# Odd transforms summed from PSUM and block evictions moved between engines, in a Fourier transform with a feed-forward layer behind it

## The chip, the cores and the metric

One core of a Trainium2 chip runs the whole kernel. The metric is the device time of one execution in microseconds. Engines by the names of the profile: PE (TensorE, products), DVE (VectorE), ACT (ScalarE), POOL (GpSimd), and SP, whose queue issues most of the transfers.

## The reference

```python
X = np.fft.fft(x, axis=1)             # x: 8 batches x 3072 positions x 256 features, float32
X = np.fft.fft(X, axis=2).real
h = X.reshape(8 * 3072, 256) @ w_in   # 256 x 2048
g = np.maximum(h, 0.0) + alpha * np.minimum(h, 0.0)
y = g @ w_out                         # 2048 x 256
```

So the real part of a transform over positions and features, a layer of 2048 hidden features with a slope of its own for each below zero, and a layer back to 256.

## The kernel before, in words

The transform over positions is folded by its symmetries into short cosine and sine products. For each of 8 batches, the input is first folded by sums and differences (`fold_piece`, four pieces on POOL and two on DVE), and then four even units (`unit`) and two odd units (`unit_odd`) make the values X that the layers read. X is kept as a high and a low part, four rows of 1552 columns: cosine high, cosine low, sine high, sine low. The transform over features is multiplied into w_in at the start.

An odd unit makes two transforms of two halves each, every one in a bank of PSUM (`dft`). ScalarE copies the second half of a bank to `os` (`odd_sums`), DVE adds and subtracts `os` and the first half (`both_sums`, L526), and three more operations of DVE combine the two results (L552, L554). `to_x` then writes the high part with ScalarE and the low part with POOL. For the sine unit, one row also goes to DRAM (`xcd`), to be spread over all partitions later.

The layers run in blocks of 512 columns (386 or 384 in the first and last batch). A block has 16 steps, one for each 128 hidden features. `step(s)` issues `ffn1(s + 3)` (six products into two banks), `ffn2(s)` (twelve products that accumulate in four banks, `acc[o, i]`), and `pair(s + 3)`, which turns the two banks of ffn1 into rows with their slope: DVE L697, L705 and L652, ScalarE L709 and L658 (high part), POOL L660 (low part). Each product is split in high and low parts, so three products stand for one. The first 14 steps of all do the weights too.

Four banks, in a ring (`pq`), serve ffn1, the transforms and the weights; the ring gives a bank to its next user when the last reader of the older contents is done. The other four are `acc`. Every engine works through its instructions in the order in which this code issues them.

At the last step of a block, `evacuate(g, 0)` is issued before `pair`, and `evacuate(g, 1)` behind it: ScalarE copies `acc[0, *]` and DVE `acc[1, *]` to SBUF, and SP sends each half out. In that last step ffn2 finishes acc 0 first and acc 1 in its second half. In all other steps, the first of the next block among them, its order is

```python
order = [(0, woh, H), (0, wol, H), (1, wol, H), (1, woh, H), (1, woh, L), (0, woh, L)]   # (o, weights, part), each for i = 0, 1
```

so the first product that writes acc 1 is the fifth, and the sixth writes `acc[1, 1]`.

X takes the place of a tile with inputs of the start (`before`). At row 3 of batch 0, POOL clears seven columns of all four rows of X (L906). In batch 0 the odd units stand at rows 16 and 19 (a row is one step), the fold of the next batch goes from row 20 to row 50; in the other batches the odd units stand at rows 0 and 3 and the fold goes from row 4 to 36. Towards the end of each batch `turn_rows` and `mids` prepare the operands of the next odd units, on ScalarE and POOL.

Of the kernel before, what the change touches and what calls it, by code (L numbers as in the profile page):

```python
# [9 lines left out]
F32 = mybir.dt.float32  # L10
# [7 lines left out]
ALU = mybir.AluOpType  # L18

NB, N, D, DFF = 8, 3072, 256, 2048  # L20
P = 128
KF = DFF // P
W = 384
WX = 386
WM = 512
XS, X0 = 1552, 7
SINGLE = 1537
BLOCKS = [(0, 0, 386), (0, 386, 384), (0, 770, 384), (0, 1154, 384)]
# [10 lines left out]
def _halves(v):  # L39

    return v.rearrange("p (h a) -> p a h", h=2)


def _pairs(v):

    return v.rearrange("p (a h) -> p a h", h=2)


def _place(b, kind):

    return {"ee": 0, "eo": 385, "o": 769}[kind[1:]] + (b == 0 and kind[1:] != "ee")
# [65 lines left out]
def _columns(b):  # L117

    j, i2 = np.arange(193), np.arange(192)
    n = 193 if b == 0 else 192  # L120
    i3 = np.concatenate([767 - 2 * j, 2 * j[:192], 768 - 2 * j[1:], 2 * j[1:192] - 1])
    k = [4 * (384 - j), 4 * j[:n], 4 * i2 + 2, 4 * (383 - i2) + 2, 2 * i3 + 1]
    sign = [-np.ones(193), np.ones(n), np.ones(192), -np.ones(192), (-1.0) ** i3]
    return np.concatenate(k), np.concatenate(sign)
# [9 lines left out]
def fft2_prelu_ffn(ctx: ExitStack, tc: tile.TileContext, t, outputs):  # L134
    nc = tc.nc
# [5 lines left out]
    foldp = ctx.enter_context(tc.tile_pool(name="foldp", bufs=1))  # L141
# [8 lines left out]
    st = start.enter_context(tc.tile_pool(name="st", bufs=1))  # L150

    V, S, G = nc.vector, nc.scalar, nc.gpsimd
# [9 lines left out]
    r128 = small.tile([1, NB], F32, name="r128")  # L162
    before = xp.tile([P, 4, XS], F32, tag="X", name="before")
    dummy = work.tile([P, 512], F32R, tag="hi0", name="dummy", bufs=3)
# [15 lines left out]
    xcd = dram.tile([NB, 1544], F32, name="xcd")  # L180
# [71 lines left out]
    wpart, w32 = {}, {}  # L252
# [40 lines left out]
    whole = st.tile([P, KEPT, D], F32, name="whole")  # L293
# [219 lines left out]
    def odd_sums(ps, n, m):  # L513
        os = foldp.tile([P, 193], F32, tag="os", name="os", bufs=2)[0:m, 0:n]
        S.activation(out=os, in_=ps[:, n:2 * n], func=ACTF.Copy)  # L515
        return ps, os, n, m

    def butterfly(ps, n, m, last=None):
        return both_sums(*odd_sums(ps, n, m), last=last)

    def both_sums(ps, os, n, m, pool=foldp, tag="y", last=None):
        wide, bufs = (WM, 1) if tag == "pf" else (WX, 2)
        last = last or n
        y = pool.tile([P, wide], F32, tag=tag, name="y", bufs=bufs)[0:m, 0:n + last]
        for i, (op, k) in enumerate(((ALU.subtract, n), (ALU.add, last)) if n == 193 else ((ALU.add, n), (ALU.subtract, n))):
            V.tensor_tensor(out=y[:, i * n:i * n + k], in0=ps[:, 0:k], in1=os[:, 0:k], op=op)  # L526
        return y

    def mids(b, nm):
# [7 lines left out]
    def mid_of(nm, i):  # L537
        return [m[:, i * P:(i + 1) * P] for m in middle[nm]] if nm in middle else None

    def unit_odd(b, nm, whole=True):  # L540

        z = zres[:, 1 if nm == "co" else 2]
        ps = [
            dft("ca", fold[b, "a" + nm], z, P, mid_of(nm, 0)), dft("sb", fold[b, nm][:, 3:6], None, P, mid_of(nm, 1)),
        ]
        parted = [(s, i, *split_sum(s, i)) for s, i in list(st1)]
        sums = [odd_sums(*v) for v in ps]
        for v in parted:
            split_parts(*v)
        ya, yb = (both_sums(*v, last=192) for v in sums)  # L550
        y = [foldp.tile([P, 512], F32, tag="xe" + e, name="yo")[:, 0:385] for e in "vg"]
        V.tensor_tensor(out=y[0], in0=ya, in1=yb, op=ALU.add)  # L552
        for o, n, at in ((0, 192, 1), (192, 191, 194)):
            V.tensor_tensor(out=y[1][:, o:o + n], in0=ya[:, at:at + n], in1=yb[:, at:at + n], op=ALU.subtract)  # L554
        at = _place(b, nm)
        for o, v in ((0, y[0]), (385, y[1][:, 0:383])):
            if nm == "so":
                nc.sync.dma_start(out=xcd[b:b + 1, at + o:at + o + v.shape[-1]], in_=v[0:1])
            to_x(0 if nm == "co" else 2, at + o, v, G)

    def unit(b, kind, lo_engine):
        sums = unit_mm(b, kind, pq.tile([P, 512], F32, tag="pq", name="ps"))
# [5 lines left out]
    def unit_mm(b, kind, bank=None):  # L568
        nm, o = kind[0] + "e", 0 if kind[1:] == "ee" else 3
        zr = zres[:, 0] if kind == "cee" else None  # L570
        return dft(kind, fold[b, nm][:, o:o + 3], zr, P, mid_of(nm, o // 3), bank)

    def unit_store(b, kind, lo_engine, y):
        s, at = 0 if kind[0] == "c" else 2, _place(b, kind)
        to_x(s, at, y if kind[1:] == "eo" or b == 0 else y[:, 0:385], lo_engine)
        if kind == "cee" and 0 < b < NB - 1:
            c = X0 + SINGLE + b
            lo_engine.tensor_copy(out=X[:, 0:2, c:c + 1], in_=X[:, 0:2, X0:X0 + 1].bitcast(F32))

    def to_x(s, c, v, lo_engine):  # L580
        hi, lo = (X[:, s + i, X0 + c:X0 + c + v.shape[-1]] for i in range(2))
        S.activation(out=hi, in_=v, func=ACTF.Copy)
        lo_engine.tensor_tensor(out=lo, in0=v, in1=hi.bitcast(F32), op=ALU.subtract)
# [86 lines left out]
    def ffn1(s):  # L670
# [4 lines left out]
        for q in range(2):  # L675
            t_ = pq.tile([P, 512], F32, tag="pq", name="pq")[:, 0:w]
            xh, xl = X[:, 2 * q, c:c + w], X[:, 2 * q + 1, c:c + w]
            xh, xl, out = _halves(xh), _halves(xl), _pairs(t_)
# [54 lines left out]
    acc = {}  # L733
# [34 lines left out]
    def evacuate(g, o):  # L768
        b, c, w = BLOCKS[g]
        if o == 0:  # L770
            outs[g] = outp.tile([P, 2, 2, w], F32, tag="o", name="o")
        v = outs[g]
        dst = outputs[g]
        for i in range(2):
            if o == 0:
                S.activation(out=v[:, o, i], in_=acc[o, i], func=ACTF.Copy)  # L776
            else:
                V.tensor_copy(out=v[:, o, i], in_=acc[o, i])
        nc.sync.dma_start(out=dst[:, o], in_=v[:, o])

    outs = {}
# [46 lines left out]
    sums = {0: fold_sums(0)}  # L828
# [21 lines left out]
    weights_b(1)  # L850
    weights_m(1, G)
    X = xp.tile([P, 4, XS], F32R, tag="X", name="X")
    see_sums = unit_mm(0, "see")
    cee_sums = unit_mm(0, "cee")
    x_sums = odd_sums(*x_sums)
# [4 lines left out]
    y = both_sums(*see_sums)  # L860
# [3 lines left out]
    y = both_sums(*cee_sums)  # L864
# [30 lines left out]

    for b in range(NB):
        mine = [g for g, block in enumerate(BLOCKS) if block[0] == b]
        r_odd, r_fold, r_end = (16, 20, 50) if b == 0 else (0, 4, 36)
        beside = []
        for r in range(len(mine) * KF):  # L900
            s = mine[0] * KF + r
            g, f = divmod(s, KF)
            step(s)
            if b == 0:
                if r == 3:
                    G.memset(X[:, :, X0 + SINGLE:X0 + SINGLE + 7].bitcast(F32), 0.0)  # L906
                    nc.sync.dma_start(out=er, in_=t["er"])
                if r == 9:
                    column_128_store("ceo", butterfly(*column_128_mm("ceo")))
                if r in (10, 11):  # L910
                    unit(0, ("ceo", "seo")[r - 10], G)
                if r in (12, 13):
                    if r == 13:
                        fold_128(0)
                    turn_rows(0, ("co", "so")[r - 12])
                if r == 25:
                    start.close()
                    late = ctx.enter_context(tc.tile_pool(name="late", bufs=1))
                if r in TABLE_STEPS:
                    parts_table(list(TABS)[TABLE_STEPS.index(r)])  # L920
            if f == 10:
                load_xbc(g + 1)
            q = r - r_odd
            if q in (0, 3):
                unit_odd(b, ("co", "so")[q // 3])
            if b + 1 < NB:
                if r == r_fold:
                    fold_tiles(b + 1)
                for i, e, r0, r1 in FOLDS:
                    r0, r1 = (r_fold + round(v * (r_end - r_fold)) for v in (r0, r1))  # L930
                    if r == r0:
                        by = one_by_one if e is V else spread
                        beside.append(by(fold_whole(6 * b + 6 + i, e), r0, r1))
                for x in beside:
                    next(x, None)
                if r == r_end + 1:
                    fold_rows(b + 1)
                    fold_128(b + 1)
                for nm, at in zip(("se", "ce", "co", "so"), (51, 52, 60, 62) if b == 0 else (37, 37, 44, 46)):
                    if r == at:  # L940
                        if nm[1] == "o":
                            turn_rows(b + 1, nm)
                        mids(b + 1, nm)
                for kind, at in zip(("see", "cee", "ceo", "seo"), (53, 55, 57, 58) if b == 0 else (38, 40, 41, 42)):
                    if r == at:
                        unit(b + 1, kind, G)
# [64 lines left out]
```

## Time and profile before

| | before |
|---|---|
| median of 3 runs | 1674.95 us (1674.49 to 1676.68) |
| the profiled execution | 1675.75 us |
| its span, first to last instruction | 1673.9 us |
| PE busy | 1642.9 us (98%) |
| DVE busy | 1512.8 us (90%) |
| POOL busy | 1328.4 us (79%) |
| ACT busy | 1133.8 us (68%) |

The times in the rows below are those of the profiled execution, counted from the start of its span. Products overlap, and the end of each is modelled, so a PE that is shown busy need not be at its peak; starts are what one can count on. A wait is put down to the last thing that ended it.

### The profile page before, as it was taken

The page shows a single profiled execution, that of the slowest core. Times are in us where ns is not written, and L with a number is a line of the kernel's source. Part 1 is how long each engine was busy: PE and PEld are TensorE (multiplying, and loading weights), DVE is VectorE, ACT ScalarE, POOL GpSimd, SP SyncE. Part 2 cuts the span into 40 slices and gives each one's busy share as a digit, 9 for nine tenths or more (in the row PEclk, how much of TensorE's full clock was granted, in tenths as well). Part 3 has the DMA queues.
Part 4 walks back from the last instruction along what each step waited for, and adds up shares of the span by engine and source line. Part 5 has one row for each costly group of instructions (what it writes and reads, how often), then busy time and mean ns, then how long its engine had stood idle before and what let it go on. Part 6 is the DMA issues. An engine that isn't in the chain of part 4 may idle for free.

```text
span 1673.9 us, 26326 instructions
## 1 busy us (share of the span) xinstructions
PE 1642.9 (98%) x8154; PEld 1462.0 (87%) x8154; DVE 1512.8 (90%) x2630; ACT 1133.8 (68%) x2094; POOL 1328.4 (79%) x1420
## 2 busy tenths in 40 slices
PE   8999999999999999999999999999999999999998
PEld 6778899888888888888888888888888888899998
DVE  7879998999889998999979998899988999889997
ACT  5876777666676666766676666766667666677775
POOL 2368997788878887889877898778887888776665
PEclk9999999999999999999999999999999999999999
DMA  6310120010100111001100111001010010000000
GB/s 237 134 62 6 58 69 20 7 70 26 45 26 20 57 39 33 32 24 47 67 3 32 39 45 57 26 7 70 29 42 26 20 45 31 1 31 25 25 20 20
DMA packets 25289, 69.93 MB, mean 42 GB/s; under 512 B 6174, under 2 KB 7486, under 8 KB 25150
## 3 DMA queue, kind: packets, MB, share of 16 engines
q1 hardware_dynamic: 24398, 67.80, 11.5%
q8 instruction: 65, 1.06, 0.3%
q14 instruction: 74, 0.61, 0.1%
q10 hardware_dynamic: 752, 0.45, 0.1%
HBM read 42.98 MB, written 25.25 MB: 41 GB/s over the span
## 4 chain that ended last, share of the span: by engine, by line
PE 88%; DVE 6%; POOL 2%; issue 2%; ACT 1%; DVEq 0%; POOLq 0%; ACTq 0%
PE acc L762 54%; PE pq L679 9%; PE pq L680 9%; PE pq L681 9%; PE ps L507 3%; DVE d L705 2%; PE ps L504 2%; PE acc L746 1%; DVE pf L697 1%; DVE d L652 1%; POOL lo L660 1%; PE fold L392 0%; PE ps L320 0%; DVE we L276 0%; DVE wm L280 0%
## 5 line engine op out<-in xcount | busy, mean ns | idle before, releaser
L660 POOL TENSOR_TENSOR lo<-d,hi 128x512 fp32r<-128x512 f32 (+2 forms) x804 | 973.2, 1227 | 238.8 <-ACT hi L658 234.8
L658 ACT ACTIVATE hi<-d 128x512 fp32r<-128x512 f32 (+2 forms) x804 | 482.7, 600 | 352.6 <-DVE d L652 254.0
L652 DVE SCALAR_TENSOR_TENSOR d<-d,sg,pq 128x512 f32<-128x512 f32 (+2 forms) x804 | 565.5, 703 | 11.1 <-ACT pq L709 11.1
L709 ACT ACTIVATE pq<-d,sga 128x512 f32<-128x512 f32 (+2 forms) x804 | 526.4, 656 | 48.8 <-DVE d L705 47.8
L705 DVE TENSOR_TENSOR d<-pf,pq 128x512 f32<-128x512 f32 (+2 forms) x832 | 531.1, 641 | 14.6 <-POOL lo L660 5.5
L762 PE MATMUL acc<-hi,woh 128*128 128x512 f32 (+2 forms) x1608 | 456.2, 365 | 1.5 <-ACT o L776 1.4
L762 PE MATMUL acc<-hi,wol 128*128 128x512 f32 (+2 forms) x1608 | 393.0, 364 | 0.0
L762 PE MATMUL acc<-lo,woh 128*128 128x512 f32 (+2 forms) x1608 | 393.0, 364 | 0.0
L697 DVE SCALAR_TENSOR_TENSOR pf<-xbc,w,pq 128x512 f32<-128x512 f32 (+2 forms) x416 | 298.0, 716 | 79.4 <-PE pq L681 72.4
L679 PE MATMUL pq<-X,wih 128*128 128x512 f32 (+2 forms) x832 | 315.5, 379 | 16.2 <-DVE d L652 15.2
L762 PEld LDWEIGHTS acc<-hi,woh 128*128 128x128 f32 x1608 | 298.0, 189 | 35.2 <-ACT o L776 4.1
L762 PEld LDWEIGHTS acc<-hi,wol 128*128 128x128 f32 x1608 | 295.4, 189 | 30.9
L762 PEld LDWEIGHTS acc<-lo,woh 128*128 128x128 f32 x1608 | 295.3, 189 | 30.9
L680 PE MATMUL pq<-X,wih 128*128 128x512 f32 (+2 forms) x832 | 302.6, 364 | 2.7 <-POOL X L906 2.5
L681 PE MATMUL pq<-X,wil 128*128 128x512 f32 (+2 forms) x832 | 302.5, 364 | 0.0
L679 PEld LDWEIGHTS pq<-X,wih 128*128 128x128 f32 x832 | 157.4, 189 | 47.7 <-PE pq L681 15.5
L680 PEld LDWEIGHTS pq<-X,wih 128*128 128x128 f32 x832 | 157.7, 190 | 17.2 <-POOL X L906 2.8
L681 PEld LDWEIGHTS pq<-X,wil 128*128 128x128 f32 x832 | 157.6, 189 | 15.7 <-DVE wil L337 0.3
L526 DVE TENSOR_TENSOR y<-ps,os 128x193 f32<-128x193 f32 (+3 forms) x132 | 40.5, 353 | 36.6 <-ACT os L515 35.6
L383 POOL TENSOR_TENSOR raw<-raw 128x512 f32<-128x512 f32 (+2 forms) x84 | 69.5, 827 | 0.0
L289 POOL TENSOR_TENSOR w<-we,wm 128x512 int32<-128x512 int32 x16 | 20.3, 1271 | 51.8 <-DVE wm L280 47.4
L776 ACT ACTIVATE o<-acc 128x512 f32<-128x512 f32 (+2 forms) x52 | 26.4, 559 | 25.3 <-PE acc L762 25.3
(157 smaller groups left out, 1068.9 us busy)
## 6 DMA issues: line engine op xcount, KB each, us to landing
raw<-in_xh SPq DMA_DIRECT2D x46, 512.0 KB
out<-o SPq DMA_DIRECT2D x36, 512.0 KB
raw<-in_w SPq DMA_DIRECT2D x15, 512.0 KB
xbc<-xcd SPq DMA_DIRECT2D x18, 256.0 KB
out<-o SPq DMA_DIRECT2D x10, 386.0 KB
out<-o SPq DMA_DIRECT2D x6, 384.0 KB
before<-in_xh SPq DMA_DIRECT2D x2, 512.0 KB
xbc<-xcd SPq DMA_DIRECT2D x5, 193.0 KB
```

The source lines that it names most:

```text
L383: yield size, lambda o=o, i0=i0, i1=i1, op=op: e.tensor_tensor(out=o, in0=i0, in1=i1, op=op)
L507: nc.tensor.matmul(out=ps[:, o:o + n], lhsT=lhsT, rhs=rhs, start=(mid is None and i == 0), stop=(i == len(terms) - 1 and (o > 0 or mid is ...
L652: V.scalar_tensor_tensor(out=g, in0=d, scalar=sg[:, f:f + 1], in1=ad, op0=ALU.mult, op1=ALU.max)
L658: S.activation(out=hi, in_=d, func=ACTF.Copy)
L660: G.tensor_tensor(out=lo, in0=d, in1=hi.bitcast(F32), op=ALU.subtract)
L679: nc.tensor.matmul(out=out, lhsT=wih[:, f, q], rhs=xh, start=True, stop=False)
L680: nc.tensor.matmul(out=out, lhsT=wih[:, f, q], rhs=xl, start=False, stop=False)
L681: nc.tensor.matmul(out=out, lhsT=wil[:, f, q], rhs=xh, start=False, stop=True)
L697: V.scalar_tensor_tensor(out=_pairs(pf), in0=_halves(xbc[g]), scalar=w128[:, f:f + 1], in1=_pairs(ps[0]), op0=ALU.mult, op1=ALU.add,)
L705: V.tensor_tensor(out=d, in0=pf, in1=ps[1], op=ALU.add if i else ALU.subtract)
L709: S.activation(out=ad, in_=d, func=ACTF.Copy, scale=sga[:, f:f + 1])
L762: nc.tensor.matmul(out=out, lhsT=wt[:, f, o * P:(o + 1) * P], rhs=rhs, start=(f == 0 and n[o] == 0), stop=(f == KF - 1 and n[o] == 2),)
```

## The change

1. `unit_odd`: the first transform's sum and difference are written back into its bank of PSUM, the second's to SBUF. Then two operations of 384 columns (add and subtract) combine them, each with one operand in PSUM. Before there were three, of 385, 192 and 191 columns, with both in SBUF. The columns are in another order, which the host undoes (`_columns`), and the two halves have 384 columns each. In batch 0 the results go to other tiles (`w32`) than in later batches.
2. `evacuate`: ScalarE copies all four banks of a block. Only in the last block of all DVE copies one, `acc[1, 1]`.
3. The memset of X's seven columns moves from row 3 of batch 0 to the place where X is made, ahead of the first values.
4. The fold of batch 1 begins at row 16 in place of 20, and still ends at 50.

```diff
-    i3 = np.concatenate([767 - 2 * j, 2 * j[:192], 768 - 2 * j[1:], 2 * j[1:192] - 1])
+    i3 = np.concatenate([2 * i2, 767 - 2 * i2, 2 * i2 + 1, 766 - 2 * i2])
...
-    def both_sums(ps, os, n, m, pool=foldp, tag="y", last=None):
+    def both_sums(ps, os, n, m, pool=foldp, tag="y"):
         wide, bufs = (WM, 1) if tag == "pf" else (WX, 2)
-        last = last or n
-        y = pool.tile([P, wide], F32, tag=tag, name="y", bufs=bufs)[0:m, 0:n + last]
-        for i, (op, k) in enumerate(((ALU.subtract, n), (ALU.add, last)) if n == 193 else ((ALU.add, n), (ALU.subtract, n))):
-            V.tensor_tensor(out=y[:, i * n:i * n + k], in0=ps[:, 0:k], in1=os[:, 0:k], op=op)
+        y = pool.tile([P, wide], F32, tag=tag, name="y", bufs=bufs)[0:m, 0:2 * n]
+        for i, op in enumerate((ALU.subtract, ALU.add) if n == 193 else (ALU.add, ALU.subtract)):
+            V.tensor_tensor(out=y[:, i * n:(i + 1) * n], in0=ps[:, 0:n], in1=os, op=op)
         return y
...
-        ya, yb = (both_sums(*v, last=192) for v in sums)
-        y = [foldp.tile([P, 512], F32, tag="xe" + e, name="yo")[:, 0:385] for e in "vg"]
-        V.tensor_tensor(out=y[0], in0=ya, in1=yb, op=ALU.add)
-        for o, n, at in ((0, 192, 1), (192, 191, 194)):
-            V.tensor_tensor(out=y[1][:, o:o + n], in0=ya[:, at:at + n], in1=yb[:, at:at + n], op=ALU.subtract)
+        halves = []
+        for k, (p, os, n, m) in enumerate(sums):
+            y = foldp.tile([P, WX], F32, tag="y", name="y", bufs=2) if k else p
+            V.tensor_tensor(out=y[:, n:2 * n], in0=p[:, 0:n], in1=os, op=ALU.subtract)
+            V.tensor_tensor(out=y[:, 0:n], in0=p[:, 0:n], in1=os, op=ALU.add)
+            halves.append(y[:, 0:2 * n].rearrange("p (k n) -> p k n", k=2))
         at = _place(b, nm)
-        for o, v in ((0, y[0]), (385, y[1][:, 0:383])):
+        for o, e, op in ((0, "v", ALU.add), (1, "g", ALU.subtract)):
+            if b:
+                y = foldp.tile([P, 512], F32, tag="xe" + e, name="yo")[:, 0:W]
+            else:
+                y = st.tile([P, 512], F32, tag="w32", name="yo", bufs=2)[:, 0:W]
+            a, c = (v[:, :, o:o + 192] for v in halves)
+            V.tensor_tensor(out=y.rearrange("p (k n) -> p k n", k=2), in0=a, in1=c, op=op)
+            c = at + o * W
             if nm == "so":
-                nc.sync.dma_start(out=xcd[b:b + 1, at + o:at + o + v.shape[-1]], in_=v[0:1])
-            to_x(0 if nm == "co" else 2, at + o, v, G)
+                nc.sync.dma_start(out=xcd[b:b + 1, c:c + W], in_=y[0:1])
+            to_x(0 if nm == "co" else 2, c, y, G)
...
         for i in range(2):
-            if o == 0:
+            if g == len(BLOCKS) - 1 and o == i == 1:
+                V.tensor_copy(out=v[:, o, i], in_=acc[o, i])
+            else:
                 S.activation(out=v[:, o, i], in_=acc[o, i], func=ACTF.Copy)
-            else:
-                V.tensor_copy(out=v[:, o, i], in_=acc[o, i])
...
     X = xp.tile([P, 4, XS], F32R, tag="X", name="X")
+    G.memset(X[:, :, X0 + SINGLE:X0 + SINGLE + 7].bitcast(F32), 0.0)
...
-        r_odd, r_fold, r_end = (16, 20, 50) if b == 0 else (0, 4, 36)
+        r_odd, r_fold, r_end = (16, 16, 50) if b == 0 else (0, 4, 36)
...
                 if r == 3:
-                    G.memset(X[:, :, X0 + SINGLE:X0 + SINGLE + 7].bitcast(F32), 0.0)
                     nc.sync.dma_start(out=er, in_=t["er"])
```

## Rows read from the trace of the kernel before

**Rows 1.** The page's first part: busy us (share of span) and instructions, PE's

```profile
PE 1642.9 (98%) x8154; PEld 1462.0 (87%) x8154; DVE 1512.8 (90%) x2630; ACT 1133.8 (68%) x2094; POOL 1328.4 (79%) x1420
```

**Rows 2.** Stretches: length, busy us of each engine (instructions), PE clock, DMA share, GB/s

```profile
165.00:235.00 70.00, 65.35 (x384) 61.60 (x383) 64.79 (x128) 48.90 (x94) 69.06 (x87) 1.00 0.18 62
360.00:410.00 50.00, 50.00 (x233) 43.77 (x233) 47.83 (x77) 32.32 (x52) 45.82 (x51) 1.00 0.11 38
```

**Rows 3.** Waits in the whole span: who <- for whom: us, times, longest us

```profile
PE pq L679 <- DVE d L652: 15.2, 35, 1.2
...
PE pq L680 <- POOL X L906: 2.5, 1, 2.5
```

**Rows 4.** Waits from 100 to 240 us (batch 0, blocks 1 to 3)

```profile
PE pq L679 <- DVE d L652: 8.6, 14, 1.2
```

**Rows 5.** Timeline at a border of two blocks: start, us, engine, line, idle before

```profile
353.10 1.08 ACT L776 ACTIVATE o<-acc 128x512 f32<-128x512 f32 x2 [1.55 <-PE acc L762]
...
354.56 1.28 DVE L778 COPY o<-acc 128x512 f32<-128x512 f32 x2
...
355.73 0.69 ACT L709 ACTIVATE pq<-d,sga 128x512 f32<-128x512 f32 x1
...
356.14 1.03 PE L762 MATMUL acc<-hi,wol 128*128 128x512 f32 x4
```

**Rows 6.** Timeline at a border of two batches and the odd unit behind it

```profile
485.61 1.03 PE L762 MATMUL acc<-hi,wol 128*128 128x512 f32 x4
...
486.77 0.69 ACT L709 ACTIVATE pq<-d,sga 128x512 f32<-128x512 f32 x1
...
490.73 1.16 DVE L526 TENSOR_TENSOR y<-ps,os 128x193 f32<-128x193 f32 x4
...
494.26 0.38 PE L679 MATMUL pq<-X,wih 128*128 128x512 f32 x1
```

**Rows 7.** Groups by line: form, count, busy us, mean ns, idle before

```profile
L552 DVE TENSOR_TENSOR yo<-y 128x385 f32<-128x385 f32 x16 | 18.6, 1165 | 0.5
L554 DVE TENSOR_TENSOR yo<-y 128x192 f32<-128x192 f32 (+1 forms) x32 | 21.2, 701 | 0.0
L705 DVE TENSOR_TENSOR d<-pf,pq 128x384 f32<-128x384 f32 x96 | 52.4, 548 | 6.6 <-POOL lo L660 5.0 <-PE acc L762 0.6
L709 ACT ACTIVATE pq<-d,sga 128x386 f32<-128x386 f32 x132 | 76.4, 580 | 5.2 <-DVE d L705 4.7 <-PE pq L681 0.5
L709 ACT ACTIVATE ad<-d,sga 128x386 f32<-128x386 f32 x28 | 15.8, 610 | 9.8 <-DVE d L705 9.7
```

**Rows 8.** Line 552 alone: duration in ns, min/median/max

```profile
L552 DVE TENSOR_TENSOR yo<-y x16: 571/1226/1943, 125.9 to 1496.0; 128x385 f32<-128x385 f32 x16
```

**Rows 9.** Timeline around the memset of X, steps 3 to 5

```profile
54.62 0.41 PE L679 MATMUL pq<-X,wih 128*128 128x386 f32 x1
...
59.09 0.41 PE L679 MATMUL pq<-X,wih 128*128 128x386 f32 x1
...
61.84 0.12 POOL L906 MEMSET X<- 128x28 f32 x1
...
68.03 0.41 PE L679 MATMUL pq<-X,wih 128*128 128x386 f32 x1
```

**Rows 10.** The stretch behind the memset, columns as in rows 2

```profile
62.00:64.00 2.00, 1.99 (x6) 1.75 (x7) 0.95 (x2) 0.00 (x0) 0.09 (x1) 0.60 0.80 238
```

**Rows 11.** Timeline of POOL and of ACT where X's first values are made

```profile
25.06 1.27 POOL L289 TENSOR_TENSOR w<-we,wm 128x512 int32<-128x512 int32 x1 [3.36 <-DVE wm L280]
...
26.07 0.53 ACT L582 ACTIVATE X<-y 128x386 fp32r<-128x386 f32 x1 [1.04 <-DVE y L526]
```

**Rows 12.** Timeline of the last evictions

```profile
1668.36 0.88 ACT L776 ACTIVATE o<-acc 128x386 f32<-128x386 f32 x2 [2.60 <-PE acc L762]
...
1669.34 1.03 DVE L778 COPY o<-acc 128x386 f32<-128x386 f32 x2 [4.22 <-PE acc L762]
```

More of the change, by code (lines that the diff above doesn't have):

```diff
@@ L516, in odd_sums, with butterfly @@
         return ps, os, n, m
-    def butterfly(ps, n, m, last=None):
-        return both_sums(*odd_sums(ps, n, m), last=last)
-    def both_sums(ps, os, n, m, pool=foldp, tag="y", last=None):
+    def butterfly(ps, n, m):
+        return both_sums(*odd_sums(ps, n, m))
+    def both_sums(ps, os, n, m, pool=foldp, tag="y"):
         wide, bufs = (WM, 1) if tag == "pf" else (WX, 2)
-        last = last or n
-        y = pool.tile([P, wide], F32, tag=tag, name="y", bufs=bufs)[0:m, 0:n + last]
-        for i, (op, k) in enumerate(((ALU.subtract, n), (ALU.add, last)) if n == 193 else ((ALU.add, n), (ALU.subtract, n))):
-            V.tensor_tensor(out=y[:, i * n:i * n + k], in0=ps[:, 0:k], in1=os[:, 0:k], op=op)
+        y = pool.tile([P, wide], F32, tag=tag, name="y", bufs=bufs)[0:m, 0:2 * n]
+        for i, op in enumerate((ALU.subtract, ALU.add) if n == 193 else (ALU.add, ALU.subtract)):
+            V.tensor_tensor(out=y[:, i * n:(i + 1) * n], in0=ps[:, 0:n], in1=os, op=op)
         return y
@@ L538, in mid_of, with unit_odd @@
         return [m[:, i * P:(i + 1) * P] for m in middle[nm]] if nm in middle else None
-    def unit_odd(b, nm, whole=True):
+    def unit_odd(b, nm):
         z = zres[:, 1 if nm == "co" else 2]
```

## Prediction

> **What bounds the kernel now.** I read the page's busy shares first, then the engines' busy time by stretch, then the waits of PE, and last the timeline at four places. PE is busy for 98% of the span [rows 1], and in a stretch inside a batch it is busy for all 50 us of 50 at full clock while DVE, ACT and POOL all have time to spare [rows 2]. So from batch 1 on the products set the pace, and an edit to another engine is worth only what PE waits for that engine. In batch 0 it is otherwise: from 165 to 235 us PE is busy for 65.35 us of 70, DVE for 64.79 and POOL for 69.06 [rows 2]; there three engines are nearly full and PE waits for what comes late. The waits name the two causes that the change can touch: PE waits for a bank that DVE's L652 frees (15.2 us in 35 waits), and once, for 2.5 us, for the memset of X [rows 3]. These idle times are shorter than what is lost, since a product is shown as 0.38 us long although the next one starts 0.217 us later (four take 1.03 us, [rows 5]): each wait costs about 0.16 us more than its idle time. In the window of batch 0 there are 14 of the 35 waits with 8.6 us [rows 4], so 8.6 + 14 x 0.16 = **10.8 us** there, and 6.6 + 21 x 0.16 = **10.0 us** in the later batches, nearly all at the odd units that open each batch.
>
> **Odd units.** Four sums of 193 columns stay four (before: two of them had 192). Of the three operations behind them, one of 385 columns takes 1.165 us in the mean and the two narrow ones 0.701 us each [rows 7], 2.57 us a unit. All three read two SBUF operands, and the time of the widest runs from 0.571 to 1.943 us [rows 8], so most of it is waiting inside the instruction while POOL works. The new operations read one operand from PSUM. The nearest row is L705, 384 columns with one PSUM operand, 0.548 us in the mean [rows 7]; I take 0.55, with 0.57 to 1.165 as the other end if they are held up like L552. That is 1.10 us for 2.57, or 1.47 us of DVE in each of 16 units. No row shows DVE writing to PSUM, as the first pair of sums now does; the nearest are ScalarE's L709 writing to PSUM (0.580 us) and to SBUF (0.610 us) at 386 columns [rows 7], so I count nothing, with 0.03 us either way for each. [...]
>
> The new wait is for the bank: the first operand's bank comes free behind both wide operations and not behind the second sum. In the unit at 490 us the four sums run from 490.73 for 1.16 us; two wide ones end at about 493.0, and the ring of four gives that bank to the product at 494.26 [rows 6]. It is covered with 1.2 us to spare, so it costs nothing.
>
> What does the saving give? Behind a late unit DVE has 1.47 us less in the same queue, and the last eviction ahead of it takes 1.28 us less (below). The waits of batches 1 to 7 are each at most 0.6 us including the hidden part, so I take **-10.0 us**, all of them. In batch 0 POOL is full as well, and the fold that starts at row 16 in place of 20 only spreads the same work over 34 rows instead of 30; nothing in it disappears, and its first sums now run beside the odd units of rows 16 and 19, which is why these take other tiles. I take half, **-5.4 us**, bounds 0 and -10.8.
>
> **Evictions on ScalarE.** This is the part that decides. ScalarE's queue in the last step of a block holds: the evictions of acc 0, then L658, L709, L658, L709 of the step three ahead, and, new, the evictions of acc 1. The copies of acc 1 that DVE issued at 354.56 [rows 5] ran while ScalarE was in the middle of that list. In the order of the code the new ones start when the second L709 is done: at 355.73 + 0.69 = 356.42, less the 0.1 us by which neighbours overlap, so 356.32, and two of them take 1.08 us like the pair at 353.10 [rows 5], until 357.40. ScalarE can't start sooner, since it began this list only when PE finished acc 0 (it was idle for 1.55 us before 353.10). PE needs acc 1 earlier: the four L762 with wol start at 356.14, 0.217 us apart, and the last two write acc[1,0] and acc[1,1] [rows 5], so acc[1,1] is due at 356.79. PE waits until 357.40 + 0.05 = 357.45: **0.66 us lost**, in a stretch where PE has no slack. Twelve borders between 512-column blocks look the same: 7.9 us. Three borders of the last batch have narrower evictions (two in 0.88 us, [rows 12]) but products that come sooner too; I estimate 0.75 us each: 2.3 us.
>
> At the seven borders between batches ScalarE is later still, because turns and splits for the next unit stand in front. At 484 us its second L709 runs from 486.77, as long as the other, until 487.46; the evictions would last until 488.44, while acc[1,1] is due at 485.61 + 3 x 0.217 = 486.26 [rows 6]: **2.23 us lost**. Five such borders give 11.2 us; the two that touch narrower blocks I estimate at 2.0 us: 4.0. The three borders inside batch 0 get 0.65 us each, 1.9 us. Sum: 7.9 + 2.3 + 11.2 + 4.0 + 1.9 = **+27.3 us**. Queued behind the waiting product are the rest of ffn2 and the next ffn1, so DVE waits too; nothing hides it. The transfer of acc 1's half is issued on SP behind the copies, one to two microseconds later; what stands behind it there are loads for steps to come, so I count nothing. Bounds: 15 us if ScalarE is a microsecond ahead at the batch borders and batch 0 hides its three; 39 us if the clock falls as well (rivals).
>
> **Memset of X.** PE's step that began at 59.09 lasted until 68.03, 8.94 us, and the one before it 4.47 (54.62 to 59.09, [rows 9]). In between POOL's memset came at 61.84, behind its other work, and the products with X's second row waited for it; the granted clock was then 0.60 [rows 10], so part of the loss came after the wait. All of the 4.47 us is the memset's. Moved ahead, it stands on POOL behind the operation that ends at 25.06 + 1.27 = 26.33, and ScalarE's first write to X, which ran at 26.07 [rows 11], must wait for it: up to 0.4 us late at the start, bounds 0 and 0.5. Sum **-4.1 us**.
>
> **End.** DVE's last two copies take 1.03 us [rows 12]; shared by two engines they take about 0.55: **-0.45 us**. The copies for the host's new column order cost nothing on the chip.
>
> **Sum.** +27.3 - 10.0 - 5.4 - 4.1 - 0.45 = +7.4 us. The profiled execution took 1675.75 us (span 1673.9 and 1.85 around it), 0.8 above the median of the runs; on it the change gives 1683.1, on the median 1674.95 + 7.4 = **1682 us**.
>
> **Rivals.**
> - *DVE's relief wins (faster).* The place is the batch border: if POOL, no longer in contention with the sums, hands the turned rows over earlier, ScalarE reaches its list some 1.6 us sooner and the seven long waits shrink to 0.66 us (4.6 for 15.2), and if all of batch 0's 10.8 us go, the sum is 7.9 + 2.3 + 4.6 + 1.9 - 10.0 - 10.8 - 4.1 - 0.45 = -8.7, **1666 us**. It decides from the point where waits for acc 1 cost less than 20 us altogether. For it: POOL and DVE are both near full in batch 0 [rows 2]. Against: the twelve ordinary borders don't depend on it.
> - *Middle.* Batch 0's whole 10.8 us go and the rest holds: +2.0, **1677 us**, no change that can be told.
> - *The clock falls too.* A longer idle stretch of PE came before the only fall seen mid-kernel [rows 9, 10], and of the 4.47 us there some 1.7 came behind the wait of 2.5. At seven borders that is up to 12 us more: **1694 us**. Against: waits of up to 1.2 us [rows 3] left the clock at 1.00 in batch 0 [rows 2].
> - *The bank comes late.* If the wide operations are held up as L552 was, 1.165 us each, the bank is free at 494.2, as late as it is wanted; in a tighter unit that is 0.5 us for each of 16, +8, **1690 us**. [...]
>
> **How the numbers follow.** Forecast 1682 us: 0.60. Clock 0.07, bank 0.05, middle 0.15, relief 0.13. The range 1673 to 1692 takes in the middle case, the bank and part of the others. A measurement here can tell about 0.2% (3.3 us): slower 0.72, the same 0.14, faster 0.14.
>
> **What would show it.** In the waits after: PE acc L762 for ACT's L776 some 20 us or more in about 50 waits, at each block's first step; PE's waits for L652 nearly gone after batch 0; no wait for the memset; the two wide operations near 0.55 us without spread. I am wrong if ScalarE's evictions of acc 1 start ahead of the second L709, or if PE doesn't wait at the ordinary borders.

## The result, and the profile after

The changed kernel takes 1693.89 us (median of 4 runs, 1693.41 to 1694.24), against 1674.72 for the kernel before (4 runs, 1674.44 to 1676.68): a ratio of 1.0112, with an interval of 1.0094 to 1.0129. That is 19.2 us longer. The forecast had the direction, 7 us of it, and a range that ended at 1692. The profiled execution took 1693.41 us with a span of 1691.6; before it was 1673.9, so 17.7 us are to be found in the traces.

The change moves the lines: L652 of before is L659 now, L679 to L681 are L686 to L688, L709 is L716, L762 is L769, and all copies out but one are ScalarE's at L785 (DVE's was L778 before). The sums of the odd units are L552 and L553, the wide operations L562.

The first part of the page, busy us, share of the span and instructions of each engine; PE's line answers [rows 1]:

```profile
PE 1653.9 (98%) x8154; PEld 1469.5 (87%) x8154; DVE 1471.2 (87%) x2563; ACT 1152.2 (68%) x2145; POOL 1327.8 (78%) x1420
```

DVE lost 42 us of work, ScalarE gained 18, and the kernel is longer. ScalarE is busy for only 68%, so a full engine is not what is wrong; e8 below tests that.

PE's waits in the whole span (who waits for whom: us, times, longest), the answer to [rows 3]:

```profile
PE acc L769 <- ACT o L785: 19.2, 27, 1.8
PE pq L686 <- DVE d L659: 7.4, 11, 2.5
PE ps L320 <- POOL w L289: 3.9, 2, 2.2
```

The wait for the memset is gone, the 15.2 us for DVE's L652 are 7.4, and a new wait of 19.2 us stands on top. From 100 to 240 us, the answer to [rows 4], nearly all that is left of DVE's share is found, and little of the new wait:

```profile
PE pq L686 <- DVE d L659: 7.0, 10, 2.5
PE acc L769 <- ACT o L785: 1.1, 3, 0.4
```

An ordinary border of two blocks, the answer to [rows 5], in the timeline (start, us, engine, line, idle before):

```profile
352.21 1.09 ACT L785 ACTIVATE o<-acc 128x512 f32<-128x512 f32 x2 [1.55 <-PE acc L769]
...
353.18 0.63 ACT L665 ACTIVATE hi<-d 128x512 fp32r<-128x512 f32 x1
...
353.70 0.69 ACT L716 ACTIVATE pq<-d,sga 128x512 f32<-128x512 f32 x1
...
354.31 0.63 ACT L665 ACTIVATE hi<-d 128x512 fp32r<-128x512 f32 x1
...
354.83 0.69 ACT L716 ACTIVATE pq<-d,sga 128x512 f32<-128x512 f32 x1
...
355.24 0.59 PE L769 MATMUL acc<-hi,wol 128*128 128x512 f32 x2
...
355.45 1.08 ACT L785 ACTIVATE o<-acc 128x512 f32<-128x512 f32 x2
...
356.09 0.97 PE L769 MATMUL acc<-hi,wol 128*128 128x512 f32 x2 [0.25 <-ACT o L785]
...
356.58 0.19 PEld L769 LDWEIGHTS acc<-hi,wol 128*128 128x128 f32 x1 [0.30 <-ACT o L785]
...
356.90 0.59 PE L769 MATMUL acc<-hi,woh 128*128 128x512 f32 x2
```

This is ScalarE's queue as the prediction read it from the code: acc 0's two copies, two pairs of L665 and L716, and only then acc 1's. From the first copy to acc 1's it is 3.24 us; the prediction had 3.22.

A border of two batches, the answer to [rows 6]:

```profile
484.63 0.31 ACT L482 ACTIVATE mh<-fso 128x128 fp32r<-128x128 f32 x1 [0.66 <-POOL fso L449]
...
484.85 1.07 ACT L785 ACTIVATE o<-acc 128x512 f32<-128x512 f32 x2
...
488.07 1.07 ACT L785 ACTIVATE o<-acc 128x512 f32<-128x512 f32 x2
...
488.71 0.97 PE L769 MATMUL acc<-hi,wol 128*128 128x512 f32 x2 [1.82 <-ACT o L785]
```

Here a split for the next unit stands in front, all of ScalarE's list comes later, and PE sits idle for 1.82 us at once.

The odd units' operations and the copies by form (line, form, count, busy us, mean ns, idle before), the answer to [rows 7]:

```profile
L785 ACT ACTIVATE o<-acc 128x512 f32<-128x512 f32 x72 | 38.9, 594 | 18.7 <-PE acc L769 18.7
...
L562 DVE TENSOR_TENSOR yo<-ps,y 128x384 f32<-128x384 f32 x32 | 16.4, 553 | 0.5
...
L552 DVE TENSOR_TENSOR ps<-ps,os 128x193 f32<-128x193 f32 x16 | 5.9, 367 | 11.9 <-ACT os L515 11.9
...
L552 DVE TENSOR_TENSOR y<-ps,os 128x193 f32<-128x193 f32 x16 | 5.7, 359 | 5.8 <-ACT os L515 5.8
```

The wide operations take 553 ns where 0.55 us was assumed. Writing a sum into PSUM takes 367 ns, and into SBUF 359: next to nothing, as assumed.

**Where the time lies.** The starts of the first ffn1 product of each block divide the span into the start with block 0 and 25 more blocks. The middle column is the first experiment below, the changed kernel with DVE's copies put back; so the two differences separate the rest of the change from the copies. Sums are in us.

| part of the span | before | e1 | after | e1 - before | after - e1 |
|---|---|---|---|---|---|
| start and block 0 | 106.81 | 103.77 | 103.90 | -3.04 | +0.13 |
| blocks 1 to 3 (batch 0) | 166.78 | 164.98 | 167.17 | -1.80 | +2.19 |
| block 4 (first batch border) | 69.16 | 67.35 | 70.79 | -1.81 | +3.44 |
| 12 blocks behind an ordinary border | 775.26 | 775.26 | 784.74 | 0.00 | +9.48 |
| 5 blocks behind a batch border | 346.95 | 338.57 | 351.47 | -8.38 | +12.90 |
| block 22 (last batch border) | 57.03 | 55.56 | 59.38 | -1.47 | +3.82 |
| blocks 23 to 25 (narrow, the end) | 151.89 | 151.88 | 154.16 | 0.00 | +2.28 |
| span | 1673.9 | 1657.4 | 1691.6 | -16.5 | +34.2 |

### The profile page after: what moved, and what is told of

The parts are those of the page before. It is cut to its first block, busy times and chain, and to the rows that moved or that the text cites. A ratio compares the mean times of both kernels' runs of the same rounds, so it can differ in the third digit from the quotient of the medians.

```text
span 1691.6 us, 26265 instructions
## 1 busy us (share of the span) xinstructions
PE 1653.9 (98%) x8154; PEld 1469.5 (87%) x8154; DVE 1471.2 (87%) x2563; ACT 1152.2 (68%) x2145; POOL 1327.8 (78%) x1420
## 4 chain that ended last, share of the span: by engine, by line
PE 84%; ACT 6%; POOL 4%; DVE 3%; issue 2%; DMA 1%; SPq 0%; ACTq 0%; POOLq 0%; DVEq 0%
PE acc L769 51%; PE pq L686 9%; PE pq L688 8%; PE pq L687 8%; PE ps L507 3%; ACT pq L716 2%; POOL lo L667 2%; ACT o L785 2%; PE acc L753 2%; PE ps L504 2%; ACT hi L665 2%; PE ps L320 1%; DVE pf L704 1%; DVE d L659 0%; DVE d L712 0%
## 5 line engine op out<-in xcount | busy, mean ns | idle before, releaser
L665 ACT ACTIVATE hi<-d 128x512 fp32r<-128x512 f32 (+2 forms) x804 | 482.9, 601 | 364.7 <-DVE d L659 302.5
L659 DVE SCALAR_TENSOR_TENSOR d<-d,sg,pq 128x512 f32<-128x512 f32 (+2 forms) x804 | 565.1, 703 | 20.4 <-ACT pq L716 20.4
L716 ACT ACTIVATE pq<-d,sga 128x512 f32<-128x512 f32 (+2 forms) x804 | 527.0, 656 | 47.6 <-DVE d L712 45.5
L769 PE MATMUL acc<-hi,woh 128*128 128x512 f32 (+2 forms) x1608 | 457.5, 366 | 1.5 <-ACT o L785 1.4
L769 PE MATMUL acc<-hi,wol 128*128 128x512 f32 (+2 forms) x1608 | 407.2, 369 | 17.9 <-ACT o L785 17.8
L769 PE MATMUL acc<-lo,woh 128*128 128x512 f32 (+2 forms) x1608 | 395.6, 366 | 0.0
L769 PEld LDWEIGHTS acc<-hi,wol 128*128 128x128 f32 x1608 | 296.2, 189 | 63.6 <-ACT o L785 33.7
L769 PEld LDWEIGHTS acc<-hi,woh 128*128 128x128 f32 x1608 | 298.9, 189 | 34.8 <-ACT o L785 4.1
L769 PEld LDWEIGHTS acc<-lo,woh 128*128 128x128 f32 x1608 | 297.4, 190 | 31.5
L686 PE MATMUL pq<-X,wih 128*128 128x512 f32 (+2 forms) x832 | 313.0, 376 | 8.1 <-DVE d L659 7.4
L688 PE MATMUL pq<-X,wil 128*128 128x512 f32 (+2 forms) x832 | 302.5, 364 | 0.0
L686 PEld LDWEIGHTS pq<-X,wih 128*128 128x128 f32 x832 | 158.0, 190 | 28.8 <-DVE d L659 5.0
L687 PEld LDWEIGHTS pq<-X,wih 128*128 128x128 f32 x832 | 158.1, 190 | 15.2 <-issue 0.5
L688 PEld LDWEIGHTS pq<-X,wil 128*128 128x128 f32 x832 | 157.8, 190 | 15.5
L785 ACT ACTIVATE o<-acc 128x512 f32<-128x512 f32 (+2 forms) x103 | 52.3, 562 | 25.7 <-PE acc L769 25.6
L383 POOL TENSOR_TENSOR raw<-raw 128x512 f32<-128x512 f32 (+2 forms) x84 | 69.3, 825 | 0.0
L525 DVE TENSOR_TENSOR y<-ps,os 128x193 f32<-128x193 f32 (+3 forms) x68 | 21.1, 352 | 30.9 <-ACT os L515 30.9
```

The costliest lines, as they stand in the source:

```text
L383: yield size, lambda o=o, i0=i0, i1=i1, op=op: e.tensor_tensor(out=o, in0=i0, in1=i1, op=op)
L659: V.scalar_tensor_tensor(out=g, in0=d, scalar=sg[:, f:f + 1], in1=ad, op0=ALU.mult, op1=ALU.max)
L665: S.activation(out=hi, in_=d, func=ACTF.Copy)
L686: nc.tensor.matmul(out=out, lhsT=wih[:, f, q], rhs=xh, start=True, stop=False)
L687: nc.tensor.matmul(out=out, lhsT=wih[:, f, q], rhs=xl, start=False, stop=False)
L688: nc.tensor.matmul(out=out, lhsT=wil[:, f, q], rhs=xh, start=False, stop=True)
```

## The experiments

**Theory A**: the loss is the place of acc 1's copies in ScalarE's queue, and the rest of the change is a gain. **Rival B**: another part loses too (odd units, bank, earlier fold), and the copies are only a share. Four kernels take the change apart.

**e1, the change with DVE's copies of acc 1 put back.**

```diff
-            if g == len(BLOCKS) - 1 and o == i == 1:
-                V.tensor_copy(out=v[:, o, i], in_=acc[o, i])
-            else:
+            if o == 0:
                 S.activation(out=v[:, o, i], in_=acc[o, i], func=ACTF.Copy)
+            else:
+                V.tensor_copy(out=v[:, o, i], in_=acc[o, i])
```

> The changed kernel with one part undone: DVE copies acc 1 again, as in the kernel before. Theory A (ScalarE's late copies of acc 1 are what makes the change slower): the 28 us that PE waits for them in the changed kernel (12 x 0.69, 3 x 0.79, 5 x 2.26, 2 x 2.1 and 2.3 in batch 0) and the three falls of the clock that stand right behind such waits (286, 890, 1494 us; about 1.5 each) go, so it takes 1694 - 28 - 4.5 = about 1661 us; up to 1668 if DVE's copies bring back some of the waits for L652 at the odd units. Rival B (the loss sits in the rest: the odd unit's operand in PSUM, or the fold that starts earlier): it stays above 1680 us.

Measured: 1659.33 us, ratio 0.9902 (0.9886 to 0.9919) to the kernel before. B is out: without ScalarE's copies the change is 15.6 us faster than before, and the copies cost 34.6 us on top of it. Whether it is their place in the queue or ScalarE's load that costs this, e7 and e8 decide. PE's waits here:

```profile
PE pq L686 <- DVE d L659: 6.7, 12, 2.0
...
PE acc L769 <- ACT o L783: 1.4, 2, 0.7
```

The second row stood in before too, with the same 1.4 us in 2 waits: acc 0 of two blocks. All else of the 19.2 us is acc 1's.

**e2, the kernel before with only the copies moved** (the inverse of that diff, on before).

> The kernel before with one part of the change alone: ScalarE copies all blocks but the last bank. Theory A: +28 us of waits for acc 1, plus 0 to 6 us of falls of the clock, minus up to 10 us of waits for L652 at the odd units that the freed DVE saves: 1692 to 1705 us, and ACT's L776 as the releaser of PE's acc products in every block. Rival B: within 5 us of 1675.

Measured: 1698.4 us, 1.0138 (1.0123 to 1.0153), so 23.4 us lost; 12 ordinary borders at 0.79 each are in it, as in after. At the batch borders it is less: a block there takes 70.55 for 69.39, only 1.16 more, against 2.37 (67.64 to 70.0) where the odd units are changed. PE's waits:

```profile
PE acc L762 <- ACT o L778: 18.7, 26, 1.8
PE pq L679 <- DVE d L652: 10.4, 21, 1.9
```

Of the wait for DVE, 10.4 us in 21 are left of 15.2 in 35. The wait for acc 1 comes ahead of it and can take part of it away, and DVE has been freed of its copies; e2 doesn't tell these two apart. Where the old wait is gone already, the new one counts in full. So the parts don't add up: alone they are worth +23.4, -14.7 and -2.5 us (e2 to e4), +6.2, and together +19.2.

**e3, the odd units alone** (the change without the copies, the memset and the earlier fold).

> The kernel before with the odd units' part alone (operand in PSUM, two wide operations, the new order of columns, the other tiles in batch 0); evictions, memset and the fold's row 20 as before. Theory A and the forecast: DVE gets 1.47 us back in each of 16 units, so the waits for L652 of batches 1 to 7 (10 us) go in large part and up to 3 us in batch 0: 1663 to 1668 us. Rival B (the bank is held too long, or a sum written to PSUM is slow): 1675 us or more, with waits of PE for the wide operations.

Measured: 1660.23 us, 0.991 (0.9895 to 0.9925), a gain of 14.7 us on 1674.97, the median of the 13 runs of before that were made beside it. Each batch-border block takes 67.63 for 69.38. Waits of PE:

```profile
PE pq L686 <- DVE d L659: 7.5, 14, 1.2
```

Of these 7.2 us in 13 waits lie between 100 and 240 us: in the later batches the waits for DVE are all but gone, and in batch 0 they are nearly untouched, 7.2 for 8.6 [rows 4].

**e4, the memset alone.**

> The kernel before with the memset of X moved alone. By the step of 8.94 us against 4.47 it gains 4.1 us: 1671 us. By the changed kernel's first block, which was 2.5 us shorter, with the clock at half for 10.2 us of the start instead of 3.4, it gains 2 to 3 us: 1672 us. If what follows the wait only takes its place, 1675 us.

Measured: 1672.49 us over 10 runs (1670.68 to 1676.14), 0.9984 (0.9975 to 0.9994): 2.5 us, not 4.1. The wait for X is gone. The profiled execution took 1676.14, the longest of the ten, and its trace shows both sides. Start and block 0 take 102.88 us, 3.9 less than before. Blocks 1 to 3 take 171.12, 4.3 more, with one wait for DVE of 4.7 us and a fall of the clock behind it:

```profile
PE pq L679 <- DVE d L652: 17.8, 31, 4.7
PE ps L320 <- POOL w L289: 5.8, 3, 2.5
```

So one trace doesn't price this edit. Over all the traces of the study, start and block 0 take 102.88 to 103.90 us in the nine kernels with the memset ahead (mean 103.46), and 104.87 to 106.81 in the three without (before, e2 and e3, mean 105.84): 2.4 us, which is what the ten runs have.

**e5 and e6: does the earlier fold harm?** In after, one of DVE's fold sums in batch 0 (L383) took 3.48 us instead of some 0.75, and PE waited for what stood behind it. Theory C: with the fold from row 20 as before, some 3 us come back. Rival D: it moves things about and comes to nothing. e5 is the change with that number alone:

```diff
-        r_odd, r_fold, r_end = (16, 16, 50) if b == 0 else (0, 4, 36)
+        r_odd, r_fold, r_end = (16, 20, 50) if b == 0 else (0, 4, 36)
```

> The changed kernel with the fold of batch 1 from row 20 again. Theory C (the earlier fold is a loss of its own: one sum of DVE took 3.48 us behind three operations of POOL, PE then waited 2.6 us and the clock fell behind it): about 4 us less than the changed kernel, 1690 us, and no fold sum of DVE over 1.3 us. Rival D (the fold's start does nothing for the total, other waits of batch 0 take its place): 1693 to 1695 us.

Measured: 1694.03 us (1691.27 to 1695.41), 1.0108 (1.009 to 1.0125). The long sum is gone, and the time is the same as far as four runs can tell, which lie 4.1 us apart; C's 1690 is below all of them. The rows of L383 in after and then in e5 (ns min/median/max):

```profile
L383 DVE TENSOR_TENSOR xev<-raw x16: 683/758/3484, 8.7 to 1379.3; 128x512 f32<-128x512 f32 x16
```

```profile
L383 DVE TENSOR_TENSOR xev<-raw x16: 683/754/893, 8.2 to 1377.5; 128x512 f32<-128x512 f32 x16
```

Blocks 1 to 3 are 1.6 us shorter in e5's trace (165.58 for 167.17). Later in it the clock falls at blocks 13, 19 and 22, and in after at blocks 4, 13 and 22; e5's 13 and 19 take 71.58 and 71.4, where such blocks otherwise take 70.0.

But the long sum doesn't come from the earlier fold. A DVE fold sum of 2.97 to 5.35 us stands in seven of the twelve traces, with the fold from row 16 (after, e1, e7, e10) and from row 20 (e2, e4, e9). It is missing in e8, whose fold begins at row 16. Behind each of the seven PE waits for DVE, 1.87 to 4.71 us, and the clock falls; in the other five traces no fall comes in batch 0 behind 100 us. The longest of these rows in e2 (fold from row 20) and of DVE's L383 on `xev` in e8 (from row 16):

```profile
L383 DVE TENSOR_TENSOR fse<-raw x32: 214/419/3572, 11.3 to 1440.8; 128x64 f32<-128x64 f32 x32
```

```profile
L383 DVE TENSOR_TENSOR xev<-raw x16: 684/790/1384, 8.5 to 1355.1; 128x512 f32<-128x512 f32 x16
```

e6 is e5 with DVE's copies of acc 1 back, except that ScalarE shares the last two.

> The changed kernel with DVE's copies of acc 1 back (in the last block ScalarE takes one of the two), and the fold from row 20. Theory C: the odd units' part alone took 1660.2 us; the memset adds -2.5 and the shared end -0.45: 1657.3 us, 2 us under the same with the fold from row 16 (1659.3). Rival D: 1659 us.

Measured: 1658.45 us (1657.68 to 1658.83), 0.9897 (0.9882 to 0.9912). It is the fastest kernel of the study, 16.5 us under before, and 0.9 us from e1, which the two sets of runs don't separate.

**e7, acc 1 wanted later.** If the place in the queue is the price, it can be paid from the other side: in the first step of a block PE does its six pairs of acc 0 and acc 1 one after the other, as it already does in the last step, so that acc 1 is due later.

```diff
-        if f == KF - 1:
+        if f in (0, KF - 1):
```

> The changed kernel, but in the first step of a block PE also does acc 0's six products first and acc 1's behind them, as in the last step; acc[1,1] is due 0.43 us later (two products). Theory A (PE waits because ScalarE's copy of acc 1 ends after PE is due there): each of 15 ordinary borders loses 0.43 to 0.46 us less, each of 7 batch borders 0.43: 9 to 10 us less, 1684 us. Rival E (the engine's load and not the due time counts): no change, 1694 us.

Measured: 1678.2 us over 10 runs, 1.0017 (1.0008 to 1.0027), 15.7 us better than after where 10 were expected. The border is as forecast: ordinary blocks go from 62.95 to 62.51 and from 67.84 to 67.40, 0.43 each, batch borders from 70.0 to 69.57. Most of the rest is in the clock, below. Its waits:

```profile
PE acc L769 <- ACT o L785: 10.9, 9, 1.4
PE pq L686 <- DVE d L659: 8.3, 11, 2.8
```

**e8, the same copies on ScalarE in another place.** Load or place? Here ScalarE does exactly the work it does in after, but acc 1's copies are issued ahead of the pair of that step:

```diff
-        if s + LEAD <= NSTEP:
-            pair(s + LEAD, early, late)
         if s >= 0 and f == KF - 1:
             evacuate(g, 1)
+        if s + LEAD <= NSTEP:
+            pair(s + LEAD, early, late)
```

> The changed kernel, but ScalarE's copies of acc 1 are issued right behind those of acc 0, ahead of the step's L665 and L716, so ScalarE does the same work in another order. Theory A (the place in ScalarE's queue is the price, not the copies themselves): at an ordinary border they end at about 355.7 where PE is due at 356.6, so PE waits for acc 1 no more; the rows come 1.2 us later, and the banks that they free are just in time: 1660 us, within 5. Rival E (ScalarE's load counts): the wait moves to L659 and the banks, 1685 us or more.

Measured: 1663.78 us, 0.9929 (0.9914 to 0.9944): 30.1 us less than after. The first part of its page:

```profile
PE 1641.6 (99%) x8154; PEld 1463.4 (88%) x8154; DVE 1479.8 (89%) x2563; ACT 1156.0 (70%) x2145; POOL 1325.3 (80%) x1420
```

ScalarE is as busy as in after, with the same 2145 instructions, and the loss is gone. An ordinary border in its timeline:

```profile
345.65 1.08 ACT L785 ACTIVATE o<-acc 128x512 f32<-128x512 f32 x2 [1.55 <-PE acc L769]
...
346.94 1.08 ACT L785 ACTIVATE o<-acc 128x512 f32<-128x512 f32 x2 [0.21 <-PE acc L769]
...
347.91 0.63 ACT L665 ACTIVATE hi<-d 128x512 fp32r<-128x512 f32 x1
```

Acc 1 is empty at 348.02, ahead of the first product that wants it, and ordinary blocks are back at 62.16 and 67.05. What remains against e6 is at the batch borders, 68.45 for 67.63: there the copies now stand ahead of the pairs, and the pairs come later. That this is what costs them is inferred from the order: no wait of PE shows it.

**e9, e8 with the fold from row 20.**

> The changed kernel with ScalarE's copies of acc 1 ahead of the step's rows, and the fold of batch 1 from row 20. If the fold's start is neutral (as between the changed kernel and its version with row 20, 1693.9 and 1694.0 us): 1664 us, like the same with row 16. If the earlier fold loses in a kernel without waits for acc 1 (1659.3 against 1658.5 with DVE's copies): 1662 to 1663 us. To beat 1658.5, DVE's 33 us of copies would have to matter in batch 0.

Measured: 1665.26 us (1663.19 to 1666.87), 0.9939 (0.9922 to 0.9955); no better than e8. Here e9's trace has one of the long fold sums (4.10 us) and e8's has none.

**e10, DVE copies acc 1 at batch borders only.** This prices the two kinds of border apart.

```diff
-            if g == len(BLOCKS) - 1 and o == i == 1:
+            if o == 1 and (i == 1 if g == len(BLOCKS) - 1 else BLOCKS[g + 1][0] != b):
                 V.tensor_copy(out=v[:, o, i], in_=acc[o, i])
```

> The changed kernel, but DVE copies acc 1 of the last block of each batch (7 blocks); ScalarE copies those of all other blocks, behind the rows. Theory A: what stays is 12 x 0.79 and 3 x 0.81 at ordinary borders and 2.3 in batch 0 on top of the 1659 us with DVE's copies everywhere: 1672 to 1674 us, and with no wait of PE longer than about 1.5 us behind batch 0 the clock doesn't fall after 250 us. If the ordinary borders are what makes the clock fall, or cost more in the queue than is seen at them: over 1677 us.

Measured: 1671.97 us over 10 runs, 0.9984 (0.9974 to 0.9993), 21.9 us less than after. Batch-border blocks take 67.63, as with DVE, and ordinary ones 62.95 and 67.84, as in after. Its waits for acc are what the ordinary borders alone make:

```profile
PE pq L686 <- DVE d L659: 7.3, 11, 2.5
PE acc L769 <- ACT o L785: 6.7, 20, 0.7
```

## Why the prediction was right, and where it was wrong

**What bounds the kernel, and the mechanism: right.** "In the order of the code the new ones start when the second L709 is done" is what the timeline shows, at the time given; e1, e7, e8 and e10 show that the place of these copies is the loss, and that nothing hides it. "Some 20 us or more in about 50 waits" were 19.2 us in 27: one at each of the 25 borders, and the two of acc 0 that stood in before too.

**Ordinary and narrow borders: mechanism right, size a little low.** 0.66 us was forecast for each of twelve, and 0.79 measured (9.48 for 7.9). The timeline above has the working. The second product of the pair was due 0.217 us after the first, whose due time was 355.24 + 2 x 0.217 = 355.67, so at 355.89; the copies end at 356.53, and with 0.05 us of handing over it starts at 356.58, together with its weight load, which has waited too. That is 0.69 us late, near the forecast. The next product then starts at 356.90, 0.32 us behind it and not 0.217: 0.10 us more, 0.79 together. In before the load of the product at 357.00 starts at 356.79, well ahead of it. That the late load makes the 0.10 is read from these rows; no run separates it. The three narrow ones and the end came to +2.28, where 2.3 - 0.45 was forecast; sharing the last copies gave 0.15 us (57.61 to 57.46 in e6), as the copy is not all that stands at the end.

**Batch borders: right.** 2.23 us forecast, 2.37 between e10 and after (67.63 to 70.0), the same 0.1 more. The two that touch narrow blocks were estimated at 2.0 each without a working; they cost 3.44 and 3.82, of which 1.2 and 1.6 are falls of the clock (next paragraph), so 2.2 each without.

**The clock: a rival that was left out of the sum, and the step that cost most.** The prediction gave a fall of the clock behind the new waits a chance of 0.07 and nothing in the sum, on the ground that waits of up to 1.2 us in batch 0 had left it alone. But its own sum made seven waits of about 2 us. The stretch behind such a wait in after, with one of batch 0 that is used below, and, in a second fence, the same border in e8 (length, busy us of each engine with instructions, granted clock, DMA share, GB/s):

```profile
890.00:894.00 4.00, 3.72 (x9) 2.86 (x10) 2.83 (x5) 3.49 (x7) 3.24 (x4) 0.57 0.32 131
...
186.00:190.00 4.00, 3.67 (x14) 3.71 (x15) 4.00 (x9) 2.70 (x6) 3.08 (x3) 0.66 0.00 0
```

```profile
890.00:894.00 4.00, 4.00 (x24) 3.84 (x23) 3.37 (x6) 3.12 (x7) 3.79 (x3) 1.00 0.02 4
```

In after the granted clock is 0.50 for most of these 4 us (0.50 from 890.5 to 893.5, 0.57 in the mean), in e8 it is 1.00. After has three such falls at border waits (286, 890 and 1494 us). The block with the one at 890 took 71.49, its neighbours without one 69.99: **1.5 us**. Block 4 took 70.79, and 69.57 in e5, where it has no fall: **1.2 us**. Block 22 took 59.38; e7 has no fall there and took 57.36, which with the 0.43 us that e7 saves at each batch border makes 57.79: **1.6 us**. (In e2 it took 59.17 with the clock at 1.00, but two of the old waits for DVE, 0.7 us, stand in it.) So the three falls cost about **4.3 us**. The fall comes at some of these waits, not all: after, e2 and e5 have 21 waits at batch borders, of 1.56 to 1.83 us, and seven falls at them. e7, e8 and e10, with no wait for acc above 1.4 us, show none between 200 us and the end, and of e7's 5.7 us beyond the forecast these falls are 4.3. The rival's 1694 us is what was measured, but by luck: it had 12 us for the falls and all the rest of the sum right.

**DVE's relief in the later batches: right, and a bit more.** -10.0 forecast; e1 has -11.7 in the blocks behind batch borders (1.81 + 8.38 + 1.47). 0.55 us for a wide operation was right, with 547 to 559 ns in 32 of them, where L552, with both operands in SBUF, ran from 571 to 1943 [rows 8]. The bank was never waited for.

**Batch 0: the other step that failed.** Half of 10.8 us was to go, "I take half, -5.4 us". Blocks 1 to 3 lost 1.8 us in e1 and 2.25 in e3 (166.78 to 164.53), and 3.3 at most, in e8. PE's wait names DVE, but what DVE waits for most there is POOL. The row of before and that of e3, from 100 to 240 us:

```profile
DVE d L705 <- POOL lo L660: 5.0, 7, 1.1
```

```profile
DVE d L712 <- POOL lo L667: 5.0, 7, 1.1
```

These 5.0 us are the same with the odd units' shorter sums. From 165 to 235 us POOL is busy for 69.06 us of 70 in before [rows 2] and for the same 69.06 in e3, and the change takes nothing from POOL. The prediction had that number in its first part and still took the middle between nothing and all. No run took work from POOL to show what that would give. What moves batch 0 from trace to trace is the long fold sum of e5's section. In after:

```profile
180.40 1.97 POOL L667 TENSOR_TENSOR lo<-d,hi 128x384 fp32r<-128x384 f32 x2
...
180.65 3.48 DVE L383 TENSOR_TENSOR xev<-raw 128x512 f32<-128x512 f32 x1 [0.60 <-DMA raw<-in_xh]
...
182.31 1.27 POOL L383 TENSOR_TENSOR xeg<-raw 128x512 f32<-128x512 f32 x1
...
185.24 0.43 PE L686 MATMUL pq<-X,wih 128*128 128x384 f32 x1 [2.47 <-DVE d L659]
```

DVE's sum, with both operands in SBUF, lasts until 184.13, behind three operations of POOL, the last of which ends at 183.58; PE waits, and then the clock falls (the row of 186 us above). e1 has such a sum and a fall too, so after's +2.19 for blocks 1 to 3 doesn't price it.

**The memset: mechanism right, size wrong.** 4.1 forecast, 2.5 measured alone (e4). "All of the 4.47 us is the memset's" is the step that failed: that stretch was read in one trace, and before's start was the longest of the three that have the memset in its old place. In e3's trace PE waited 1.9 us for it and not 2.5, and its start is 1.94 us shorter than before's. Behind this wait, from 62 to 66 us, the granted clock is 0.57 in before and 1.00 in e2 and e3: before's 4.47 us held a fall that the wait doesn't always bring. The 0.4 us put down for ScalarE's first write to X didn't come: it starts at 25.63, and the memset at 25.83.

**The sum.** Forecast +7.4. Of the missing 10.3 us of the span, 7.4 are in the copies (34.24 for 27.3 - 0.45): 4.3 in the three falls, which the sum had at nothing, 1.6 at the ordinary borders, 0.5 at the two beside narrow blocks, 0.2 at the other batch borders, and 0.4 each in batch 0 and at the narrow ones. The other 3.0 are in the rest (-16.5 for -19.5): 3.6 too much for batch 0 and 1.1 for the start, against 1.7 too little for the later batches. All errors but that last one went the same way.

## What to carry to other kernels

Before a copy goes to another engine, write out that engine's queue around it, and put the copy's end against the moment its reader is due: busy share says nothing, for the same 2145 instructions of ScalarE took 1694 us in one order and 1664 in another. A gain on an engine counts only where the waits name that engine and no other stands full beside it; where two are full, count the gain of one as small: here 1.8 to 3.3 us of 10.8, and not half. And a sum that makes waits longer than any that the trace has behind its start must carry the clock as a term, and not as a remote rival.

## What the runs showed of the hardware

At an ordinary border a product that waited in the middle of a pair cost 0.10 us more than the wait: its weight load waited too and started with it at 356.58, and the next product came at 356.90, 0.32 us behind it for the usual 0.217. A DVE sum with two SBUF operands lasted 3.48 us in after (at 180.65) and 2.97 in e1 (at 125.5), where the median of such sums is 0.76 and 0.69; in after, three operations of POOL in a row ran beside it. In before, L554, also with both operands in SBUF, took (ns min/median/max)

```profile
L554 DVE TENSOR_TENSOR yo<-y x32: 342/347/1431, 127.8 to 1497.4; 128x192 f32<-128x192 f32 x16, 128x191 f32<-128x191 f32 x16
```

The 20 with no operation of POOL beside them took 342 to 348 ns, the 12 with one 1153 to 1431. Of L552's 16, ten took 1216 to 1943 ns, and each ended 416 to 420 ns behind an operation of POOL; the other six took 571 to 582 ns with POOL at work too, so POOL's work alone doesn't tell them apart. The wide operations of after, with one operand in PSUM, kept within 547 to 559 ns, with POOL at work beside all 32. The clock fell at seven of the 21 waits for acc of 1.56 to 1.83 us, and behind 200 us in no run at one of up to 1.4 us; what tells the waits with a fall from those without one stays open.
